# Attention with a one in the denominator, then a two-layer Mish block: how the first twelve head pairs and the first product are laid out

## The chip, the cores and the metric

The kernel runs on one core of one Trainium2 chip. The metric is the device time of one execution in microseconds; smaller is better. Three executions of the kernel before were timed. The profile is of one execution.

## The reference

`q`, `k` and `v` are 8 batches x 12 heads x 448 rows x 64, in float32; `w_in` is 768 x 2048 and `w_out` 2048 x 768.

```python
scores = scale * np.matmul(q, k.transpose(0, 1, 3, 2))
m = np.max(scores, axis=-1, keepdims=True)
e = np.exp(scores - m)
attn = e / (np.sum(e, axis=-1, keepdims=True) + np.exp(-m) + 1e-09)
attn_out = np.matmul(attn, v)
x = attn_out.transpose(0, 2, 1, 3).reshape(B * S, H * D)   # 3584 x 768
h = x @ w_in
sp = np.where(h > 20.0, h, np.log1p(np.exp(np.minimum(h, 20.0))))
out = (h * np.tanh(sp)) @ w_out                            # Mish, then the second product
```

## The kernel before

**Units of work.** Two heads make a pair: 6 pairs a batch, 48 pairs in all, numbered 0 to 47. Three pairs make a unit. The order of all instructions on each engine is written by hand: every engine takes its instructions in the order in which the Python code issues them, so a call made earlier stands earlier in that engine's queue.

**One pair.** `load_pair` issues three DMAs on SP's queue (L120). `cast_pair` makes bf16 copies on POOL (L161 to L163). `transpose_pair` turns q and k on PE (L178) into a PSUM tile, and `evac_qk` copies both out (L197 and L217 on ACT, or L199 and L215 on DVE; from pair 12 on, q goes out on DVE by L209 in a block-diagonal layout). Scores come in 4 steps a pair (`STEPS`), seven row tiles of 128 in all: two tiles in each of steps 0 to 2 and one in step 3. `scores` runs the matmuls (L254 to L265, later L248) into one of three score tiles in PSUM and then the negated row maximum on DVE (L269). `exps` runs the exponentials on ACT with their row sums (L282), and after a pair's last step a small exponential of the negated maxima (L289). `scores_ahead` keeps three steps in flight: the step that comes three later is issued after the exponentials of the present one have been issued, and uses the score tile that they free.

**Normalising and turning.** `denominators` (L295, L299, DVE) gives one over the sum; `normalise` multiplies the seven tiles in place, on DVE (L316), or on POOL (L314) after a copy of the factors (L307). The result must be turned before it is multiplied with v: by one DMA transpose on SP's queue (L320), or for the pairs in `BY_PE` by PE: `turn_on_pe(p, j)` does seven transposes (L331) into one of two PSUM tiles `mo`, and a DVE copy (L335) follows later. `av_pair` is the product with v (L357), its copy into `xT` (L366) again follows later. "Later" means a queue `late` in Python, emptied by `flush_late`, which issues the pending copies at that place. `mo_take` hands out the two `mo` tiles and empties `late` if none is free.

**The two products.** `mm1_mish` does six matmuls of `w_in` with `xT` (L381) for one of 16 blocks of 128 columns, then Mish on ACT (L387). The second product is dealt out in chunks of two matmuls (L436, `mm2_part`), which a unit's steps interleave with the scores; `plan` says which parts go into which unit. From unit 4 on (pair 12) each unit has such filler.

**Order before.** Pairs 0 to 5 run in a loop of their own, step by step, with no other PE work than attention. In it, at pair p: step 0 issues the loads of p+4, the casts of p+3, one piece of weights and the denominators of p-1; step 1 the copies of q and k of p+2 and the normalising of p-1 with its DMA transpose; step 3 the transposes of p+3 and the product with v of p-3. Then come units 2 and 3 (pairs 6 to 8 and 9 to 11), each followed by eight of batch 0's sixteen first-product blocks, with normalising, score steps and transposes of the next unit between them. Pairs 5, 6 and 7 are turned by PE, at most one turn a step. From unit 4 on the loop is the same to the end: twelve steps with filler of the second product, then eight blocks of a first product.

**Weights.** 20 pieces are loaded with a cast by DMAs that POOL issues (L147): 12 of `w_in` (256 rows x 512 columns each), 8 of `w_out`.

Of the kernel before, what the change touches and what calls it, by code (L numbers as in the profile page):

```python
# [19 lines left out]
def kernel(  # L20
# [15 lines left out]
    NT = 4  # L36
# [50 lines left out]
    for t_ in en_bufs:  # L87
# [140 lines left out]
    def scores(idx):  # L228

        p, s = divmod(idx, STEPS)  # L230
        if s == 0:
            if p < HP or p % UNIT_PAIRS == 0:
                for nm in ("negm", "sums", "expm", "den", "rden"):
                    stats[nm] = st_pool.tile([128, UNIT_PAIRS, NTILE], FP32, tag=nm, name=nm)
            at = 0 if p < HP else p % UNIT_PAIRS
            att[p] = {nm: t[:, at, :] for nm, t in stats.items()}
            att[p].update(en=en_bufs[p % N_EN], whole=dict(stats))
# [36 lines left out]
    def exps(idx):  # L274
# [6 lines left out]
        for bk, c in enumerate(cols):  # L281
# [5 lines left out]
            )  # L287
        if s == STEPS - 1 and p < HP:
# [12 lines left out]
    def normalise(p, dma=True, on_pool=False):  # L301
# [6 lines left out]
        for i in range(NTILE):  # L308
            args = dict(
                out=en[:, :, i, 0:SP_], in0=en[:, :, i, 0:SP_],  # L310
                scalar1=st["rden2" if on_pool else "rden"][:, i : i + 1],
            )
            if on_pool:
                nc.gpsimd.tensor_scalar(scalar2=1.0, op0=ALU.mult, op1=ALU.mult, **args)  # L314
            else:
                nc.vector.tensor_scalar(scalar2=None, op0=ALU.mult, **args)  # L316
        eT = eT_pool.tile([128, NT, 2 * S], BF16, tag="eT", name="eT")
        st["eT"] = eT
        if dma:
            nc.sync.dma_start_transpose(  # L320
                out=eT.rearrange("c j (i q) -> c (j i) q", q=128),
                in_=en.rearrange("q j i c -> q (j i c)"),
            )

    def turn_on_pe(p, j, act=False):
# [47 lines left out]

    def mm1_mish(b, ff):
        if ff == 0:
            gT[b] = gT_pool.tile([128, FF_T, S], BF16, tag="gT", name="gT")
        flush_late()
        spare = ff % FF_U == 2
        h_ps = sc_tiles[0][:, 0, :] if spare else mo_take()
# [97 lines left out]
    LOAD_AT = (0, 3, 6)  # L477
    HEAD = HP
# [13 lines left out]
    load_pair(3)  # L492
    cast_pair(2)


    for p in range(HEAD):
        for s in range(STEPS):
            if s == 1 and p == 0:
                transpose_pair(p + 2)
            exps(p * STEPS + s)  # L500
            if p == 0 and s == 0:
                evac_qk(1, act=True)
            if s == 1:
                evac_qk(p + 2, act=True)
            if s:
                flush_late()
            scores_ahead(HEAD * STEPS + 3)
            if s == (2 if p == HEAD - 1 else 0):
                load_pair(p + 4)
            if s == 0:  # L510
                cast_pair(p + 3)
                load_w(1)
                if p:
                    denominators(att[p - 1])
            if s == 1:
                if p:
                    normalise(p - 1)
            if s == 3 and p + 3 < HEAD + 2:
                transpose_pair(p + 3)
            if s == 3 and p >= 3:  # L520
                av_pair(p - 3, act=True)
    denominators(att[HEAD - 1])
    normalise(HEAD - 1, dma=HEAD - 1 not in BY_PE)

    for u in range(UNITS_PER_B, N_UNITS + 2 * UNITS_PER_B):
        attn = u < N_UNITS
# [9 lines left out]
        for n in range(steps):  # L536
            pi, s = divmod(n, STEPS)
            p, idx = p0 + pi, p0 * STEPS + n
            late_tp = u == UNITS_PER_B and n == STEPS
            if late_tp:  # L540
                transpose_pair(p0 + 2)
            exps(idx)
            if late_tp:
                evac_qk(p0 + 2)
            if u == UNITS_PER_B + 1 and n == 0:
                for j in range(2):
                    turn_on_pe(HEAD, j)
            flush_late()
# [10 lines left out]
            early = AV_AT.get(u - UNITS_PER_B)  # L559
            if early is not None:  # L560
                if n in early:
                    av_pair(early[n])
                for pe, n0 in BY_PE.items():
                    first = 2 if pe == HEAD else 0
                    if pe // UNIT_PAIRS == u - 1 and n0 + first <= n < n0 + NT:
                        turn_on_pe(pe, n - n0)
            elif s == (2 if pi else 0) and N_PAIRS <= p < N_PAIRS + UNIT_PAIRS:
                av_pair(p - UNIT_PAIRS)
            if u - UNITS_PER_B < len(W_AT):
                load_w(W_AT[u - UNITS_PER_B].get(n, 0))  # L570
        assert done == total
# [3 lines left out]
        nxt = p0 + UNIT_PAIRS  # L575
        todo = sorted(range(p0, nxt), key=lambda p: p in BY_PE)
        for f in range(FF_U):
            if moe:
                mm1_mish(b, w * FF_U + f)
            if u == UNITS_PER_B and f in (2, 6) or u == UNITS_PER_B + 1 and f == 1:  # L580
                load_w(1)
            if not attn:
                continue
            if f == 0:
                denominators(att[p0]["whole"])
                normalise(todo[0], dma=todo[0] not in BY_PE)
            if f == 3:
# [6 lines left out]
            if f == 3:  # L594
                normalise(todo[1], dma=todo[1] not in BY_PE)
            if f == (4 if u >= first_mm2 else FF_U - 1):
                normalise(todo[2], dma=todo[2] not in BY_PE, on_pool=u >= first_mm2)
    flush_late()
# [31 lines left out]
```

## Time and profile before

| | us |
|---|---|
| median of 3 runs (494.7 to 497.88) | 496.76 |
| profiled execution: its time and its span | 494.7 |
| PE busy (share of the span) | 453.2 (92%) |
| PE weight loads busy | 249.9 (51%) |
| DVE busy | 349.8 (71%) |
| ACT busy | 349.1 (71%) |
| POOL busy | 151.1 (31%) |
| share of the 16 DMA engines: SP's queue, POOL's queue | 80.7%, 8.8% |

The page's chain of what ended last goes through PE for 72% of the span, DVE for 12% and ACT for 10%. Busy times are shares of the whole span; what limits a stretch has to be read from that stretch. The first exponential starts at 7.9 us, that of pair 6 at 46.7, of pair 9 at 79.7 and of pair 12 at 111.6.

### The profile page before, as it was taken

The numbers are of one execution on the slowest core, as the hardware profiler recorded it, in microseconds if no ns is written. First come the engines' busy times: TensorE is split into PE (matmuls) and PEld (weight loads), VectorE is DVE, ScalarE is ACT, GpSimd is POOL, SyncE is SP. The second block draws the span as 40 slices with busy tenths as digits, with TensorE's granted clock in tenths as the row PEclk, the third lists the DMA queues.
The fourth block names the chain that finished last, engine by engine and source line by source line (L and its number), as shares of the span: only waits on it lengthen the run. The fifth ranks groups of instructions, "written<-read, shape, count | busy, mean of one in ns | idle before, by whom it ended". The sixth has DMA issues, their size and how long they took to land.

```text
span 494.7 us, 9027 instructions
## 1 busy us (share of the span) xinstructions
PE 453.2 (92%) x3120; PEld 249.9 (51%) x3120; DVE 349.8 (71%) x706; ACT 349.1 (71%) x906; POOL 151.1 (31%) x252
## 2 busy tenths in 40 slices
PE   4466877798999999999999999999999999999996
PEld 2122433454554556555655555555555565556573
DVE  4897988788868686968878786878796878420011
ACT  5888766668787787978797878888797879502300
POOL 4622271501432424242423324242424230300000
PEclk9999997799999999999999999999999999999999
DMA  8999999979999969989998999899989696670112
GB/s 209 194 213 228 243 222 226 193 135 217 192 218 286 184 201 189 264 163 233 195 242 188 191 193 218 221 179 245 194 243 181 187 146 144 128 159 18 47 50 79
DMA packets 209453, 92.20 MB, mean 186 GB/s; under 512 B 166272, under 2 KB 205952, under 8 KB 209408
## 3 DMA queue, kind: packets, MB, share of 16 engines
q1 hardware_dynamic: 201920, 85.35, 80.7%
q0 software_dynamic: 7488, 6.29, 8.8%
q8 instruction: 24, 0.39, 0.3%
q14 instruction: 21, 0.17, 0.1%
HBM read 45.61 MB, written 11.01 MB: 114 GB/s over the span
## 4 chain that ended last, share of the span: by engine, by line
PE 72%; DVE 12%; ACT 10%; issue 2%; DMA 1%; SPq 1%; POOL 0%; DVEq 0%; ACTq 0%; POOLq 0%
PE mo L436 24%; PE mo L381 24%; ACT en L282 9%; PE sc L248 8%; DVE negm L269 6%; PE sc L357 6%; DVE en L316 3%; PE sc L381 3%; PE sc L178 3%; PE mo L357 2%; DMA k_f<-in_k_dram 1%; PE sc L254 1%; DVE xT L366 1%; PE mo L331 1%; SPq L120 1%
## 5 line engine op out<-in xcount | busy, mean ns | idle before, releaser
L282 ACT ACTIVATE en<-sc,negm 128x448 bf16<-128x448 f32 x336 | 209.2, 636 | 33.6 <-DVE negm L269 15.3
L269 DVE TENSOR_REDUCE negm<-sc 128x2 f32<-128x896 f32 x192 | 182.9, 970 | 58.4 <-PE sc L248 44.4
L436 PE MATMUL mo<-w_out_sb,gT 128*128 128x384 bf16 (+2 forms) x1152 | 167.1, 309 | 0.0
L381 PE MATMUL mo<-xT,w_in_sb 128*128 128x448 bf16 x672 | 139.8, 352 | 1.3 <-DVE xT L366 1.0
L436 PEld LDWEIGHTS <-gT 128*128 128x128 bf16 (+1 forms) x1152 | 97.3, 100 | 56.5 <-issue 5.9
L387 ACT ACTIVATE gT<-mo 128x448 bf16<-128x448 f32 x112 | 59.3, 543 | 72.6 <-PE mo L381 72.4
L381 PEld LDWEIGHTS <-w_in_sb 128*128 128x128 bf16 x768 | 72.8, 98 | 64.6 <-issue 3.7
L314 POOL TENSOR_SCALAR en<-en,rden 128x448 bf16<-128x448 bf16 x84 | 51.8, 637 | 103.4 <-DVE rden L307 69.6
L161 POOL CAST q_bf<-q_f 112x512 bf16<-112x512 f32 x47 | 28.9, 614 | 155.2 <-DMA q_f<-in_q_dram 145.8
L422 DVE COPY o_sb<-mo 128x384 f32<-128x384 f32 (+1 forms) x64 | 32.1, 502 | 60.1 <-PE mo L436 60.0
L248 PE MATMUL sc<-kT,qd 128*128 128x448 bf16 x252 | 71.7, 354 | 1.5 <-DVE qd L209 0.7
L316 DVE TENSOR_SCALAR en<-en,rden 128x448 bf16<-128x448 bf16 x252 | 69.8, 348 | 0.9
L282 ACT ACTIVATION_READ_ACCUMULATOR en<-sc,negm 128x1 f32 x336 | 69.1, 206 | 0.0
L248 PEld LDWEIGHTS <-qd 128*128 128x128 bf16 x252 | 23.5, 97 | 33.3 <-issue 16.6
L254 PE MATMUL sc<-kT,qd 64*128 64x448 bf16 x36 | 17.5, 502 | 20.4 <-ACT en L282 17.4
L357 PE MATMUL sc<-eT,v_bf 112*64 112x448 bf16 x288 | 34.0, 356 | 2.3 <-ACT en L282 1.8
L163 POOL CAST v_bf<-v_f 112x512 bf16<-112x512 f32 x48 | 29.8, 621 | 14.3 <-DMA v_f<-in_v_dram 13.4
L357 PEld LDWEIGHTS <-v_bf 112*64 112x64 bf16 x384 | 21.3, 115 | 22.8 <-issue 16.8
L162 POOL CAST k_bf<-k_f 112x512 bf16<-112x512 f32 x47 | 29.0, 617 | 5.8 <-DMA k_f<-in_k_dram 5.1
L209 DVE TENSOR_SCALAR qd<-sc 64x448 bf16<-64x448 bf16 x72 | 27.8, 386 | 0.9
L217 ACT COPY kT<-sc 128x448 bf16<-128x448 bf16 x39 | 20.8, 535 | 8.2 <-PE sc L178 8.2
L178 PEld LDWEIGHTS <-q_bf 112*128 112x128 bf16 x192 | 14.4, 104 | 16.5 <-DVE q_bf L161 4.2
(47 smaller groups left out, 275.0 us busy)
## 6 DMA issues: line engine op xcount, KB each, us to landing
q_f<-in_q_dram SPq DMA_DIRECT2D x48, 224.0 KB, 5.1
k_f<-in_k_dram SPq DMA_DIRECT2D x48, 224.0 KB, 5.2
v_f<-in_v_dram SPq DMA_DIRECT2D x48, 224.0 KB, 5.4
w_in_sb<-in_moe_w_in_dram POOLq DMA_DIRECT2D x12, 256.0 KB, 5.6
w_out_sb<-in_moe_w_out_dram POOLq DMA_DIRECT2D x8, 384.0 KB, 7.4
out_dram<-o_sb SPq DMA_DIRECT2D x7, 336.0 KB, 3.6
out_dram<-o_sb SPq DMA_DIRECT2D x8, 288.0 KB, 4.6
out_dram<-o_sb SPq DMA_DIRECT2D x8, 240.0 KB, 3.2
```

Of the source, the lines that this page charges most:

```text
L163: nc.gpsimd.tensor_copy(out=v_bf, in_=v_f)
L178: nc.tensor.transpose(by_s[s][:, t * SP_ : (t + 1) * SP_], src[:, t].rearrange("p h d -> p (h d)"), ident[:SP_, :SP_],)
L248: nc.tensor.matmul(sc[:, bk, 0:S], lhsT=qT[:, i].rearrange("d h r -> d (h r)"), rhs=kT, start=True, stop=True,)
L269: nc.vector.tensor_reduce(out=negm, in_=sc[:, 0 : len(cols), 0:S], axis=AX.X, op=ALU.max, negate=True)
L282: nc.scalar.activation(out=st["en"][:, :, c, 0:SP_], in_=sc[:, bk, 0:S].rearrange("q (j c) -> q j c", j=NT), func=AF.Exp, bias=st["negm"][ ...
L314: nc.gpsimd.tensor_scalar(scalar2=1.0, op0=ALU.mult, op1=ALU.mult, **args)
L316: nc.vector.tensor_scalar(scalar2=None, op0=ALU.mult, **args)
L357: nc.tensor.matmul(av[h * 64 : (h + 1) * 64, 0:S], lhsT=v_bf[:, h, j * D : (j + 1) * D], rhs=e_h, start=(j == 0), stop=(j == NT - 1),)
L381: nc.tensor.matmul(h_ps[:, 0:S], lhsT=w_in_sb[:, dm, ff * 128 : (ff + 1) * 128], rhs=xT[b][:, dm, :], start=(dm == 0), stop=(dm == DM_T - 1),)
L387: nc.scalar.activation(out=gT[b][:, ff, :], in_=h_ps[:, 0:S], func=AF.Mish)
L422: nc.vector.tensor_copy(out=o_sb[:, cols], in_=st["o"][:, 0:n_cols])
L436: nc.tensor.matmul(st["o"][r : r + n, 0:n_cols], lhsT=gT[bb][:, ff, c0 : c0 + n], rhs=w_out_sb[:, ff, cols], start=(ff == 0), stop=(ff == ...
```

## The change

The loop of the first pairs now takes twelve pairs (`HEAD = 2 * HP`), and the general loop starts at unit 4. After pair 6 (`MOE_AFTER`) all sixteen blocks of batch 0's first product run in one stretch; the first two, which need all of `xT`, are begun with five of six matmuls each before pair 5's product with v (`mm1_first`). The pairs turned by PE are 3, 4, 5, 7 and 8, two turns in each of steps 2 and 3 of the next pair. Normalising of pair p-1 is dealt out: tiles 4 to 6 to POOL and tiles 0 and 1 to DVE in step 0, tiles 2 and 3 to DVE in step 1. The transposes of q and k of pair p+3 move from step 3 to step 1 of pair p, their copies by ACT to step 2 of pair p. One part of the second product (16 matmuls) is spread over the steps of pairs 10 and 11, and `plan` of units 4 and 5 is cut accordingly. `w_in` comes in pieces of 128 rows x 1024 columns; the places where pieces are issued are a table by pair and step.

```diff
+    HEAD = 2 * HP
...
     def w_pieces():
-        c_in, c_out = d_ff // 4, NH
-        for i in range(4):
-            for a in range(0, DM_T, 2):
+        c_in, c_out = d_ff // 2, NH
+        for i in range(2):
+            for a in range(DM_T):
                 yield (
-                    w_in_sb[:, a : a + 2, i * c_in : (i + 1) * c_in],
-                    moe_w_in[a * 128 : (a + 2) * 128, i * c_in : (i + 1) * c_in],
+                    w_in_sb[:, a : a + 1, i * c_in : (i + 1) * c_in],
+                    moe_w_in[a * 128 : (a + 1) * 128, i * c_in : (i + 1) * c_in],
                 )
...
+    def normalise_tiles(p, tiles, on_pool=False):
+        st = att[p]
+        en = st["en"]
+        if on_pool:
+            st["rden2"] = st_pool.tile([128, NTILE], FP32, tag="rden2", name="rden2")
+            nc.vector.tensor_copy(out=st["rden2"], in_=st["rden"])
+        for i in tiles:
+            ...
+            if on_pool:
+                nc.gpsimd.tensor_scalar(scalar2=1.0, op0=ALU.mult, op1=ALU.mult, **args)
+            else:
+                nc.vector.tensor_scalar(scalar2=None, op0=ALU.mult, **args)
...
+    def mm1_first(b, banks, last):
+        gT[b] = gT_pool.tile([128, FF_T, S], BF16, tag="gT", name="gT")
+        def part(ff, dms):
+            ...
+        for ff in range(len(banks)):
+            part(ff, range(DM_T - 1))
+        last()
+        flush_late()
+        for ff in range(len(banks)):
+            part(ff, (DM_T - 1,))
+            nc.scalar.activation(out=gT[b][:, ff, :], in_=banks[ff][:, 0:S], func=AF.Mish)
...
         if g == 0:
-            plan[u0] = [(0, i, 0, 2) for i in range(2)] + [(0, 2, 0, 1)]
-            plan[u0 + 1] = [(0, 2, 1, 1)] + [(0, i, 2, 2) for i in range(3)]
+            plan[u0] = [(0, i, 0, 2) for i in (1, 2)]
+            plan[u0 + 1] = [(0, i, 2, 2) for i in range(3)]
...
-    BY_PE = {HEAD - 1: 1, HEAD: 0, HEAD + 1: STEPS}
-    AV_AT = {0: {5: 3, 7: 4, 10: 5}, 1: {3: 8, 6: 6, 10: 7}}
-    W_AT = ({5: 1, 9: 1}, {1: 1, 5: 1, 7: 1, 9: 1, 11: 1}, {1: 1, 3: 1, 5: 1, 7: 1})
+    MOE_AFTER = HP
+    BY_PE = (3, 4, 5, 7, 8)
+    ON_POOL = 3
+    W_AT = {
+        (1, 2): 1, (2, 0): 1, (2, 2): 1, (3, 0): 1, (3, 2): 1, (4, 0): 1, (4, 2): 1,
+        (5, 0): 1, (5, 2): 1, (6, 0): 1, (6, 2): 2,
+        (7, 0): 1, (8, 0): 1, (8, 2): 1, (9, 0): 1, (9, 2): 1, (10, 0): 1, (10, 2): 1,
+        (11, 0): 1,
+    }
...
+    av_with.update({p: p - UNIT_PAIRS for p in range(MOE_AFTER + 3, HEAD)})
+    early = deque(fn for fn, _ in mm2_part(0, 0, 0, 2))
     for p in range(HEAD):
         for s in range(STEPS):
...
             exps(p * STEPS + s)
-            if p == 0 and s == 0:
-                evac_qk(1, act=True)
-            if s == 1:
-                evac_qk(p + 2, act=True)
-            if s:
-                flush_late()
-            scores_ahead(HEAD * STEPS + 3)
-            if s == (2 if p == HEAD - 1 else 0):
-                load_pair(p + 4)
-            if s == 0:
-                cast_pair(p + 3)
-                load_w(1)
-                if p:
-                    denominators(att[p - 1])
-            if s == 1:
-                if p:
-                    normalise(p - 1)
-            if s == 3 and p + 3 < HEAD + 2:
-                transpose_pair(p + 3)
-            if s == 3 and p >= 3:
-                av_pair(p - 3, act=True)
+            if p == 0 and s < 2:
+                evac_qk(1 + s, act=True)
+            if s == 2:
+                evac_qk(p + 3, act=True)
+            flush_late()
+            if p >= HEAD - 2:
+                early.popleft()()
+            limit = MOE_AFTER + 1 if p <= MOE_AFTER else HEAD + 1
+            scores_ahead(limit * STEPS)
+            load_w(W_AT.get((p, s), 0))
+            if s == 0:
+                load_pair(p + 4)
+                if p - 2 in BY_PE and p <= MOE_AFTER:
+                    av_pair(p - 2, act=True)
+                if p and p - 1 != MOE_AFTER:
+                    denominators(att[p - 1])
+                    normalise_tiles(p - 1, range(NTILE - ON_POOL, NTILE), on_pool=True)
+                    normalise_tiles(p - 1, range(0, 2))
+                cast_pair(p + 3)
+            if s == 1:
+                if p and p - 1 != MOE_AFTER:
+                    normalise_tiles(p - 1, range(2, NTILE - ON_POOL))
+                    turn(p - 1, dma=p - 1 not in BY_PE)
+                transpose_pair(p + 3)
+            if s >= 2 and p - 1 in BY_PE:
+                for j in (2 * s - 4, 2 * s - 3):
+                    turn_on_pe(p - 1, j)
+            if s == 3 and 3 <= p < MOE_AFTER and p - 3 not in BY_PE:
+                av_pair(p - 3, act=True)
+        if p == MOE_AFTER:
+            denominators(att[p])
+            mm1_first(
+                0, [sc_tiles[1][:, i, :] for i in range(2)],
+                lambda: (flush_late(), av_pair(p - 1, bank=sc_tiles[2][:, 0, :])),
+            )
+            normalise(p)
+            for ff in range(2, FF_T):
+                mm1_mish(0, ff, banks=False)
+                if ff >= FF_T - 6 and ff % 2 == 0:
+                    scores_ahead((p + 1) * STEPS + (ff - FF_T) // 2 + 4)
     denominators(att[HEAD - 1])
-    normalise(HEAD - 1, dma=HEAD - 1 not in BY_PE)
+    normalise(HEAD - 1)
...
-    for u in range(UNITS_PER_B, N_UNITS + 2 * UNITS_PER_B):
+    for u in range(first_mm2, N_UNITS + 2 * UNITS_PER_B):
```

`turn` is the part of `normalise` after the multiplications: it takes the tile `eT` and issues the DMA transpose if asked to.

More of the change, by code (lines that the diff above doesn't have):

```diff
@@ L287, in exps @@
             )
-        if s == STEPS - 1 and p < HP:
+        if s == STEPS - 1 and p < HEAD:
             nc.scalar.activation(out=st["expm"], in_=st["negm"], func=AF.Exp)
@@ L316, in normalise, with turn @@
                 nc.vector.tensor_scalar(scalar2=None, op0=ALU.mult, **args)
+        turn(p, dma)
+    def turn(p, dma):
+        st = att[p]
         eT = eT_pool.tile([128, NT, 2 * S], BF16, tag="eT", name="eT")
@@ L371, in av_pair, with mm1_mish @@
         del att[p], casted[p], qkT[p]
-    def mm1_mish(b, ff):
+    def mm1_first(b, banks, last):
+        gT[b] = gT_pool.tile([128, FF_T, S], BF16, tag="gT", name="gT")
+        def part(ff, dms):
+            for dm in dms:
+                nc.tensor.matmul(
+                    banks[ff][:, 0:S],
+                    lhsT=w_in_sb[:, dm, ff * 128 : (ff + 1) * 128],
+                    rhs=xT[b][:, dm, :],
+                    start=(dm == 0), stop=(dm == DM_T - 1),
+                )
+        for ff in range(len(banks)):
[5 more added lines that the diff above has]
+            nc.scalar.activation(out=gT[b][:, ff, :], in_=banks[ff][:, 0:S], func=AF.Mish)
+    def mm1_mish(b, ff, banks=True):
         if ff == 0:
@@ L377, in mm1_mish @@
         flush_late()
-        spare = ff % FF_U == 2
+        spare = banks and ff % FF_U == 2
         h_ps = sc_tiles[0][:, 0, :] if spare else mo_take()
@@ L558 @@
                 cast_pair(p0 + LOAD_AT.index(n) + LEAD - 1)
[L559 to L567, printed above, removed]
+            if s == (2 if pi else 0) and N_PAIRS <= p < N_PAIRS + UNIT_PAIRS:
                 av_pair(p - UNIT_PAIRS)
-            if u - UNITS_PER_B < len(W_AT):
-                load_w(W_AT[u - UNITS_PER_B].get(n, 0))
         assert done == total
@@ L585 @@
                 denominators(att[p0]["whole"])
-                normalise(todo[0], dma=todo[0] not in BY_PE)
+                normalise(p0)
             if f == 3:
@@ L594 @@
             if f == 3:
[L595 to L597 removed]
+                normalise(p0 + 1)
+            if f == 4:
+                normalise(p0 + 2, on_pool=True)
     flush_late()
```

26 lines of the change are left out of this document (10 added, 16 removed).

## The prediction

> **What bounds the kernel now.** The program runs on one core and its span of 494.7 us is the time of its profiled execution; the three runs lie at 494.7, 496.76 and 497.88 us, so the sum below is made against 494.7 and 2.1 us are added at the end for the median. First I read the stretches (columns: stretch, its length, busy time of PE, PE weight loads, DVE, ACT, POOL with counts, granted clock, DMA share, GB/s).
>
> ```profile
> 7.90:46.70 38.80, 22.24 (x119) 8.63 (x116) 32.05 (x63) 34.15 (x107) 15.79 (x25) 1.00 1.12 211
> 65.70:79.70 14.00, 11.13 (x86) 6.11 (x85) 11.54 (x25) 8.34 (x16) 6.69 (x11) 1.00 1.12 179
> 111.60:126.70 15.10, 13.04 (x88) 7.25 (x87) 12.60 (x23) 13.62 (x44) 4.29 (x7) 1.00 1.01 227
> 138.60:494.70 356.10, 350.32 (x2464) 197.57 (x2462) 236.09 (x473) 246.71 (x628) 101.21 (x168) 1.00 0.83 178
> ```
>
> From 138.6 us on PE is busy for 350.32 of 356.10 us: nothing lost earlier can be made up there. Before that PE is idle for much of the time, and every microsecond won or lost ahead of the first exponential of pair 12 (111.6 us) shows at the end. The change rewrites just this part. I call the time from the first exponential of pair p to that of pair p+1 "stage p". In the timeline stages 0 to 5 start at 7.9, 14.7, 20.0, 26.8, 32.7, 40.3 us, pairs 6 to 8 take 46.7 to 65.7, pairs 9 to 11 79.7 to 99.4, and the two halves of the first product 14.0 and 12.2 us. A stage thus costs 6.4 us on average.
>
> Second, the timeline of stage 3, for what hangs on what:
>
> ```profile
> 26.80 0.67 ACT L282 ACTIVATE en<-sc,negm 128x448 bf16<-128x448 f32 x1
> 28.25 0.58 PE L262 MATMUL sc<-kT,qd 64*64 64x448 bf16 x1
> 29.93 0.54 ACT L197 ACTIVATE qd<-mo 128x448 bf16<-128x448 bf16 x1
> 30.11 0.15 DVE L295 SCALAR_TENSOR_TENSOR den<-sums,expm 128x7 f32<-128x7 f32 x1
> 30.30 0.20 DVE L299 RECIPROCAL rden<-den 128x7 f32<-128x7 f32 x1
> 31.02 0.61 POOL L161 CAST q_bf<-q_f 112x512 bf16<-112x512 f32 x1 [9.33 <-DMA q_f<-in_q_dram]
> 33.29 0.56 PE L178 MATMUL mo<-ident,q_bf 112*128 112x112 bf16 x4
> ```
>
> The denominators of pair 2 are ready 3.7 us into stage 3 (2.7 us into stage 1, at 17.40, where no turn or normalising was pending), since on DVE they stand behind the maximum of the stage's last scores, and these wait for a score tile that the stage's first exponentials free. POOL's casts wait for the load alone, and the transposes made from them are copied out by ACT only in the next stage: there is a slack of half a stage. Stages 1 to 3 are DVE's (the chain from 20 to 48 us is 24.7% L269 and 23.3% L316).
>
> **What the change does to a plain stage.** Part one: normalising is dealt out, four tiles to DVE, three to POOL. On DVE that saves three tiles of 0.26 us and adds the 0.16 us copy (L307): DVE falls to 3.7 of maxima, 0.35 and 0.16 of denominators and 1.0 of tiles, 5.2 us. But POOL's three tiles are written ahead of the casts of pair p+3 in POOL's order, and the transposes of p+3 move from step 3 to step 1 and their copies by ACT from the next stage to step 2 of the same one. What was slack is now a chain inside each stage, and ACT, which takes its work in order, stands in it. Rows for the pieces:
>
> ```profile
> 16.17 0.58 PE L262 MATMUL sc<-kT,qd 64*64 64x448 bf16 x1
> 134.55 0.16 DVE L307 COPY rden<-rden 128x7 f32<-128x7 f32 x1
> 134.88 4.33 POOL L314 TENSOR_SCALAR en<-en,rden 128x448 bf16<-128x448 bf16 x7 [6.80 <-ACT kT L217]
> 16.55 0.62 POOL L162 CAST k_bf<-k_f 112x512 bf16<-112x512 f32 x1
> 15.65 0.58 PE L178 MATMUL mo<-ident,k_bf 112*128 112x112 bf16 x4
> 30.36 0.54 ACT L217 COPY kT<-mo 128x448 bf16<-128x448 bf16 x1
> ```
>
> Two exponentials release PE after 1.4 us (12.80 to 14.21); scores 0.55 and hand-over 0.15; maximum 0.6; denominators 0.3; copy and hand-over 0.3: 3.3 us. POOL: 3 x 0.62 = 1.85; casts of q and k 1.2: 6.35. PE turns k (0.55), ACT copies it (0.1 + 0.4): 7.4; last exponential and the small one 0.7: **8.2 us**, 1.8 more than a stage costs now. ACT would otherwise have come to the copies at 3.7 us; it stands idle for some 3 us. Nothing covers this: PE's next scores are queued behind the late transposes.
>
> **Turning by PE.** Pairs 3, 4, 5, 7 and 8 get 4 x 7 PE transposes and four DVE copies each in place of one DMA transpose (before: 5, 6, 7, spread one turn a step). Rows for a turn, a copy and one pair's product with v, at the slow and at the fast pace of PE:
>
> ```profile
> 53.46 0.99 PE L331 MATMUL mo<-ident,en 128*112 128x128 bf16 x7
> 54.08 0.61 DVE L335 COPY eT<-mo 112x896 bf16<-112x896 bf16 x1
> 59.28 1.68 PE L357 MATMUL mo<-eT,v_bf 112*64 112x448 bf16 x8
> 61.37 0.95 PE L357 MATMUL mo<-eT,v_bf 112*64 112x448 bf16 x8
> 89.18 0.60 PE L331 MATMUL mo<-ident,en 128*112 128x128 bf16 x7
> ```
>
> The turns stand in steps 2 and 3, behind the transposes of p+3; their copies stand on DVE ahead of two maxima, and a product with v stands on PE ahead of the next stage's last scores. So they lengthen the stage after, 5, 6, 9 and 10, from one stage's transposes to the next stage's: at the slow pace PE's scores, two turns, scores, two turns, product, scores (0.55 + 2.0 + 0.55 + 2.0 + 1.7 + 0.55 = 7.35), maximum 0.75, denominators, copy and hand-overs 0.65, POOL 1.85, casts 1.25, transposes 0.55: 12.4 us. At the fast pace DVE carries it (scores 0.45, maximum 1.05, copies 1.2, maximum 1.05, one copy 0.6, then product 0.95, scores and maximum 1.1, and from the denominators on the same with transposes of 0.36, 4.1): 10.5 us. Which pace PE has is not to be read from the granted clock, which is 1.00 in both 50 to 60 us and 60 to 70 us, but from the durations. In this part most are slow (L254 502 ns on average, 350 where fast). I take 11.6 us.
>
> The Trainium skill, "TensorE: Matmul & The Clock Gate" (Part 4: PE-mode transpose), says that transposes don't count as PE work in releasing the full clock; by it the five turns would stay at the slow pace and these stages at 12.4 us, 3.2 us more in all. The trace leaves it open: seven took 0.99 us at 53.46 and 0.60 at 89.18, among fast matmuls.
>
> The DMA side gains (six DMA transposes ahead of pair 12 in place of eight, loads no longer behind them on SP's queue), but in the longer stages each load has landed well before its cast: POOL's 35.2 us of waiting for q_f go into the new wait. I count nothing; if that cover went, it would cost as now, 1 to 2 us in a stage.
>
> **The first product in one stretch.** It needs 96 matmuls as before. From the end of pair 6's exponentials: remaining turns 1.2 to 2.8 us, ten matmuls 2 to 3, the product of pair 5 and its copy 1.7, two matmuls 0.4, fourteen groups of 1.14 (L381: six in 1.14 to 1.30) 16.0, three scores 1.1, last Mish and table load 1.9 (109.75 to 111.63 now): 24 to 27, taken 26, against 14.0 + 12.2 = 26.2. One pair of table loads goes, but ACT has room there. Normalising pair 6 (1.8 us of DVE) hides under it.
>
> **w_in in rows of 1024.** Still 12 pieces of 256 KB, 0.73 us each to issue on POOL, where POOL waits for the denominators anyway; w_out's eight follow, three of them earlier than now. Nothing; if POOL were full, 0.7 us a piece.
>
> **The sum.** Lead-in 7.9; stage 0 8.1 (6.8 and the copies of pair 3, which wait for its k cast at 14.2); stages 1 to 3 and 8 at 8.2: 32.8; stage 4 9.0 (ACT waits for pair 0's product with v); 5, 6, 9, 10: 46.4; stage 7 5.4 (no normalising in it); stage 11 9.6 (pair 8's product with v goes first, 0.95 to 1.7); stretch 26: 145.2 against 111.6, **+33.6**. Later, sixteen 384-column matmuls (2.6 us) move out of the PE-bound part and two narrow passes become one wider: 1.8 us less in each of two units, of which the first is ACT's (13.62 of 15.10 busy): -1.8 to -3.6, taken -2.4. Together +31.2: 525.9, with 2.1 **528 us**.
>
> **Rivals.** (1) PE stays fast throughout: 42 for the four long stages, plain ones 7.8, stretch 24.5, lower bounds elsewhere: +24.9 - 3.4, 518 us. For it: 89 to 91 us; against: fast spells last 2 to 4 us there. (2) PE slow throughout, and POOL and DVE hold each other up: +40 in all, 537 us. For it: seven DVE tiles took 1.80 us at 25.86 and 2.72 at 19.05, while POOL cast; that is 0.13 a tile, 0.5 a stage. The Trainium skill, "SBUF — State Buffer" (Who interferes with whom), has the two share a port pair that one holds for a whole instruction; by it POOL's three tiles could wait for two of DVE's, also 0.5 us a stage. (3) The other side: casts don't hold ACT up. It decides at 3.7 us into a stage: if k's copy can start by then, six plain stages run at ACT's 5.6 us, the five with a turn at 6.4 (19.0 / 3 now), stretch 24.5: 106.1, -5.5 - 2.4: 489 us. For it: DVE's load falls and it bounds stages 1 to 3; against: POOL's order, and 6.35 us of measured pieces ahead. (4) The loss vanishes in slack later: 497 us; against it the 350.32 of 356.10.
>
> **Numbers.** Chances: forecast 0.58, (1) 0.20, (2) 0.12, (3) 0.06, (4) 0.04. About 1% can be told from no change; the first three are slower by more, so slower 0.90, (4) same, (3) faster. The range runs from under rival 1, where two of its stages might go at less than DVE's sum, to rival 2: 512 to 538.
>
> **What would show it.** Pair 12's first exponential near 145 us; POOL casts right behind three L314-like tiles; ACT idle about 3 us a stage ahead of its copies, released by PE's transposes; long stages 5, 6, 9, 10; PE full after pair 15. Wrong if casts run ahead of denominators, if stages 1 to 3 stay under 7 us, or the stretch under 22.

## The result, and the profile after

Four runs of the changed kernel have a median of 537.17 us (535.98 to 538.17), four of the kernel before 496.19 us. The ratio is 1.0814, its 95% interval 1.0785 to 1.0843: **slower by 41 us**. The forecast was 528, its range 512 to 538. The profiled execution took 537.87 us with a span of 536.1; the sums below go by the spans, 536.1 against 494.7. (In every run that has both numbers the time is about 1.8 us above the span. The prediction took before's span for a time and added 2.1 us for the median, which comes to nearly the same.)

The stretches of the changed kernel, in the columns of the stretches shown of before: pairs 0 to 6, the stretch of the first product, pairs 7 to 11, unit 4, and the rest.

```profile
7.85:76.30 68.45, 34.91 (x228) 18.68 (x228) 41.31 (x78) 42.07 (x128) 34.24 (x57) 0.94 0.97 167
76.30:102.39 26.09, 22.81 (x128) 11.59 (x127) 7.88 (x16) 11.38 (x20) 2.68 (x5) 0.95 0.99 190
102.39:151.07 48.68, 29.14 (x174) 14.80 (x174) 34.51 (x70) 25.65 (x83) 20.76 (x33) 0.64 0.54 88
151.07:168.00 16.93, 14.86 (x81) 7.09 (x81) 14.52 (x26) 13.59 (x45) 3.61 (x6) 0.92 0.86 202
180.00:536.10 356.10, 349.26 (x2455) 196.87 (x2453) 236.36 (x472) 246.56 (x628) 101.46 (x168) 1.00 0.80 177
```

The last line says what the forecast needed: the PE-bound part is as full as before (349.26 of 356.10 us), so the early loss shows at the end. Pair 12's first exponential stands at 151.07 us; before it stood at 111.63. Of 41.4 us of span, 39.4 are lost ahead of it and 2.0 behind. In 7.85 to 76.30 no engine is full; ACT is busy for 61%. That is the picture of a chain. Its links, in the timeline of stage 2:

```profile
24.40 0.64 ACT L283 ACTIVATE en<-sc,negm 128x448 bf16<-128x448 f32 x1
25.80 0.53 PE L263 MATMUL sc<-kT,qd 64*64 64x448 bf16 x1 [0.77 <-ACT en L283]
26.48 0.62 DVE L270 TENSOR_REDUCE negm<-sc 128x1 f32<-128x448 f32 x1 [0.26 <-PE sc L266]
27.45 0.17 DVE L335 COPY rden<-rden 128x7 f32<-128x7 f32 x1
27.80 2.05 POOL L342 TENSOR_SCALAR en<-en,rden 128x448 bf16<-128x448 bf16 x3 [3.90 <-DVE rden L335]
29.80 0.64 POOL L162 CAST q_bf<-q_f 112x512 bf16<-112x512 f32 x1
30.40 0.60 POOL L163 CAST k_bf<-k_f 112x512 bf16<-112x512 f32 x1
31.06 0.55 PE L179 MATMUL mo<-ident,k_bf 112*128 112x112 bf16 x4
31.71 0.54 ACT L198 ACTIVATE qd<-mo 128x448 bf16<-128x448 bf16 x1 [3.50 <-PE mo L179]
32.15 0.53 ACT L218 COPY kT<-mo 128x448 bf16<-128x448 bf16 x1
33.28 0.64 ACT L283 ACTIVATE en<-sc,negm 128x448 bf16<-128x448 f32 x1
```

Each line starts within 0.2 us of the end of the one above, with three steps left out (the tile's second exponential, 25.00 to 25.65, the denominators from 27.02 on, and the pair's last exponential with the small one behind it, 32.56 to 33.28), and 8.9 us go by from one first exponential to the next. The bracket on L162 is missing: its load had long landed. The waits of 0 to 152 us (total, times, longest) show the same chain, and the one wait that the forecast lacked, the last. (POOL's longest, 32.6 us, is the stretch of the first product, where it has nothing to normalise.)

```profile
POOL en L342 <- DVE rden L335: 63.2, 7, 32.6
ACT qd L198 <- PE mo L179: 24.3, 9, 4.7
ACT kT L218 <- DVE qd L210: 19.1, 3, 6.8
```

| stage | forecast, us | measured, us |
|---|---|---|
| lead-in and 0 | 16.0 | 15.50 |
| 1, 2, 3, 8 | 8.2 each | 8.90, 8.88, 9.02, 8.97 |
| 4 | 9.0 | 9.64 |
| 5, 6, 9, 10 | 11.6 each | 13.50, 10.85, 11.27, 11.76 |
| stretch | 26 | 26.1 |
| 7 | 5.4 | 5.72 |
| 11 | 9.6 | 10.96 |
| sum to pair 12 | 145.2 | 151.07 |
| behind it, against before | -2.4 | +2.0 |

The lengths look right. Whether each has the cause that it was given is for the experiments. Where they give a stage's length, it runs from the small exponential that ends one pair (L290 in the changed kernel) to the next one.

### The profile page after: what moved, and what is told of

Read it like the earlier page. It is cut to its first block, busy times and chain, and to the rows that moved or that the text cites. A ratio compares the mean times of both kernels' runs of the same rounds, so it can differ in the third digit from the quotient of the medians.

```text
span 536.1 us, 9138 instructions
## 1 busy us (share of the span) xinstructions
PE 465.8 (87%) x3160; PEld 257.1 (48%) x3160; DVE 347.4 (65%) x694; ACT 350.1 (65%) x915; POOL 169.5 (32%) x282
## 4 chain that ended last, share of the span: by engine, by line
PE 67%; DVE 9%; ACT 9%; DMA 6%; POOL 4%; issue 3%; SPq 1%; DVEq 0%; POOLq 0%; ACTq 0%
PE mo L423 23%; PE mo L478 21%; PE sc L249 7%; ACT en L283 7%; PE sc L378 6%; DVE negm L270 5%; DMA k_f<-in_k_dram 4%; PE sc L423 3%; PE sc L179 2%; POOL en L342 2%; PE mo L179 1%; PE mo L352 1%; DVE xT L387 1%; DMA out_dram<-o_sb 1%; POOL q_bf L162 1%
## 5 line engine op out<-in xcount | busy, mean ns | idle before, releaser
L283 ACT ACTIVATE en<-sc,negm 128x448 bf16<-128x448 f32 x336 | 209.6, 640 | 21.1 <-DVE xT L387 10.8
L478 PE MATMUL mo<-w_out_sb,gT 128*128 128x384 bf16 (+2 forms) x1136 | 171.1, 314 | 0.5 <-DVE eT L356 0.5
L315 POOL TENSOR_SCALAR en<-en,rden 128x448 bf16<-128x448 bf16 x84 | 52.0, 641 | 102.8 <-DVE rden L308 69.2
L283 ACT ACTIVATION_READ_ACCUMULATOR en<-sc,negm 128x1 f32 x336 | 70.4, 210 | 0.0
L162 POOL CAST q_bf<-q_f 112x512 bf16<-112x512 f32 x47 | 29.1, 619 | 97.1 <-DMA q_f<-in_q_dram 71.1
L317 DVE TENSOR_SCALAR en<-en,rden 128x448 bf16<-128x448 bf16 x182 | 47.7, 334 | 0.8
L342 POOL TENSOR_SCALAR en<-en,rden 128x448 bf16<-128x448 bf16 x30 | 20.3, 687 | 80.4 <-DVE rden L335 63.2
L378 PE MATMUL sc<-eT,v_bf 112*64 112x448 bf16 x320 | 38.6, 362 | 3.0 <-ACT en L283 2.5
L179 PE MATMUL mo<-ident,q_bf 112*128 112x112 bf16 x60 | 8.1, 289 | 36.5 <-POOL q_bf L162 32.2
L179 PEld LDWEIGHTS <-q_bf 112*128 112x128 bf16 x192 | 14.4, 107 | 48.5 <-POOL q_bf L162 37.8
L164 POOL CAST v_bf<-v_f 112x512 bf16<-112x512 f32 x48 | 29.6, 618 | 16.0 <-DMA v_f<-in_v_dram 15.4
L163 POOL CAST k_bf<-k_f 112x512 bf16<-112x512 f32 x47 | 29.1, 619 | 5.3 <-DMA k_f<-in_k_dram 4.1
L255 PE MATMUL sc<-kT,qd 64*128 64x448 bf16 x36 | 18.0, 511 | 12.4 <-ACT en L283 11.8
```

Source lines behind the costliest of these rows:

```text
L162: cast_q(out=q_bf, in_=q_f.rearrange(by_t, t=NT))
L179: nc.tensor.transpose(by_s[s][:, t * SP_ : (t + 1) * SP_], src[:, t].rearrange("p h d -> p (h d)"), ident[:SP_, :SP_],)
L283: nc.scalar.activation(out=st["en"][:, :, c, 0:SP_], in_=sc[:, bk, 0:S].rearrange("q (j c) -> q j c", j=NT), func=AF.Exp, bias=st["negm"][ ...
L378: nc.tensor.matmul(av[h * 64 : (h + 1) * 64, 0:S], lhsT=v_bf[:, h, j * D : (j + 1) * D], rhs=e_h, start=(j == 0), stop=(j == NT - 1),)
L478: nc.tensor.matmul(st["o"][r : r + n, 0:n_cols], lhsT=gT[bb][:, ff, c0 : c0 + n], rhs=w_out_sb[:, ff, cols], start=(ff == 0), stop=(ff == ...
```

## The experiments

All edits are to the changed kernel but one. A run without an interval is a single execution, so 2 us between two of them tell nothing (before ran between 494.1 and 498.2); the stages, which start and end inside one execution, are compared instead.

**Casts ahead of POOL's tiles.** Theory: the chain within a stage is the loss. Rival: moving the turns and the products is.

```diff
                 load_pair(p + 4)
+                cast_pair(p + 3)
...
                     normalise_tiles(p - 1, range(0, 2))
-                cast_pair(p + 3)
```

> The changed kernel with one call moved: the casts of pair p+3 stand ahead of POOL's three normalising tiles in POOL's order; nothing else differs. Theory (the chain inside a stage: denominators, POOL's tiles, casts, transposes, ACT's copies): ACT no longer idles 3.5 us ahead of its copies in plain stages; stages 1, 2 and 8 fall from 8.9 us to about 6, stages 3 and 4, where the loads of pairs 6 and 7 come into play, to 7 or 8, the four long stages (13.5, 10.9, 11.3, 11.8) to 8 to 10, stage 11 from 11.0 to 8; pair 12's first exponential moves from 151 to about 126 and the time from 537 to about 512 us. Rival (the turning by PE carries the loss): stages 1, 2, 3 and 8 may shorten, but the long ones stay at 10 to 13 and the time stays over 525. Rival (the slow pace of PE alone): every stage stays within 1 us, over 530.

530.21 us. Stages 1, 2 and 8 fall to 5.72 us each: the chain was what set them. But stage 3 takes 14.1 us, and only 7 us of the whole are won. In the timeline of this kernel's SP and POOL:

```profile
21.67 7.53 SPq L325 DMA_TRANSPOSE eT<-en  x1
29.26 0.56 SPq L121 DMA_DIRECT2D q_f<-in_q_dram  x1
37.86 0.61 POOL L162 CAST q_bf<-q_f 112x512 bf16<-112x512 f32 x1 [9.58 <-DMA q_f<-in_q_dram]
```

The same DMA transpose in the changed kernel:

```profile
21.16 4.37 SPq L325 DMA_TRANSPOSE eT<-en  x1
```

The cast waits 9.58 us for a load of q. SP could issue that load only at 29.26 us, behind a DMA transpose that held the queue for 7.53 us in place of 4.37, and the cast could start only 8.6 us after that. A second limit stands behind the first.

**All seven tiles on DVE**, dealt out as in the change, so that nothing of POOL's stands ahead of the casts:

```diff
-                    normalise_tiles(p - 1, range(NTILE - ON_POOL, NTILE), on_pool=True)
...
-                    normalise_tiles(p - 1, range(2, NTILE - ON_POOL))
+                    normalise_tiles(p - 1, range(2, NTILE))
```

> The changed kernel with all seven normalising tiles on DVE (two in step 0, five in step 1): POOL has only casts and DMA issues in the first twelve pairs. Theory (the chain): the casts run as soon as their loads have landed, as when they are moved ahead; DVE takes 0.8 to 1.2 us more a stage, so plain stages come to 6 to 6.5 us and the long ones to 9 to 11; about 515. Rival (DVE's relief by POOL is worth more than POOL's order costs): slower than 537, DVE full. Rival (turning carries it): over 525.

528.1 us, 13 above the expectation. Stages 1 to 3 take 5.71, 6.71 and 7.05 us; stages 4 and 6 go up to 11.7 and 11.8, and POOL now waits for q_f. The same turn of events by another edit.

**Transposes late.** The transposes of p + 3 go back to step 3 and their copies to the next stage; POOL's order stays.

```diff
-            if s == 2:
-                evac_qk(p + 3, act=True)
+            if s == 1:
+                evac_qk(p + 2, act=True)
...
-                transpose_pair(p + 3)
...
+            if s == 3:
+                transpose_pair(p + 3)
```

> The changed kernel with the transposes of pair p+3 back in step 3 and their copies by ACT back in step 1 of the next pair; POOL's tiles still stand ahead of the casts. Theory (the chain needs both, POOL's order and the early copies): with the slack of half a stage back, ACT doesn't wait: stages 1 and 2 fall from 8.9 to 6 or 6.3 us although the casts are as late as in the changed kernel; from stage 3 on the loads decide (they waited behind 7.5 to 9.5 us of DMA transposes when the casts were put first), 7 to 9 us; pair 12 starts at 120 to 135 instead of 151, the time is 508 to 523 us. Rival (POOL's order alone costs, wherever the transposes stand): stages 1 and 2 stay over 8 us, over 530 in all.

543.3 us, outside the expectation, and still it answers the question: stages 1 to 3 take 5.27, 5.39 and 5.75 us. So the chain needs both halves, POOL's order and the early copies; undoing either breaks it. The time is lost elsewhere. Pair 9's transposes now hold one of the two `mo` tiles through the stretch, which takes some 36 us, a side effect of this edit. And stage 5 takes 21.4 us, from the waits of 40 to 70 us:

```profile
ACT en L283 <- DMA eT<-en: 12.0, 1, 12.0
```

Pair 5's exponentials wait for pair 1's DMA transpose to leave their buffer; SP's row for it is 17.41 us long.

**w_in in rows of 512**, as before:

```diff
-        c_in, c_out = d_ff // 2, NH
+        c_in, c_out = d_ff // 4, NH
...
-                    w_in_sb[:, a : a + 1, i * c_in : (i + 1) * c_in],
+                    w_in_sb[:, a : a + 2, i * c_in : (i + 1) * c_in],
```

> The changed kernel with w_in in pieces of 256 rows x 512 columns again, issued at the same places. In the changed kernel the loads of pair 8 reached POOL late in stage 5 (2.5 us of waiting), while the DMA engines were busy at only 65 to 105 GB/s. Theory (the chain): the pieces cost nothing in plain stages; the time stays within 2 us of 537. Rival (the long rows crowd the loads): stage 5 falls from 13.5 to about 11 and the time to 534 or 535; if the rows carried the loss, below 525.

535.58 us: the rows cost nothing that shows. Stage 5 takes 10.8 us in it, but also 11.1 and 11.2 in two later runs that keep the long rows; the 13.50 of the profiled execution was that execution's.

**w_in not loaded.** If the crowded transfers are the second limit, taking w_in's twelve away must free stage 3 once the casts go first, and change nothing while the chain stands. Two kernels, both with

```diff
+    nc.vector.memset(w_in_sb[:, 0:4], 0.02)
+    nc.gpsimd.memset(w_in_sb[:, 4:DM_T], 0.02)
...
-                yield (
-                    w_in_sb[:, a : a + 1, i * c_in : (i + 1) * c_in],
...
+                yield None
```

the first with the casts moved as above, the second without:

> The casts stand ahead of POOL's three tiles, and w_in is not loaded: DVE and POOL set it to a constant at the start, so the values are others, and twelve transfers of 256 KB are gone. Theory: with the chain in a stage undone, the loads are the next limit, and w_in is what crowds them. Then stage 3 (14.1 us with the casts first and w_in loaded) falls under 8, stage 5 (12.8) under 10.5, POOL's wait for q_f from 29.1 us under 10, SP's DMA transposes go back from 7.5-9.5 to under 6 us each, and the time from 530.2 to 517-523 us. Rival: what is left is the order of work on DVE and PE: stages 3 and 5 stay above 12 and the time within 3 us of 530.

> The changed kernel with its order kept, and w_in not loaded (set to a constant, as in the run beside it). Theory: in the changed kernel the chain inside a stage ends last and the loads have slack behind it, so the plain stages stay at 8.8-9.0 us; only stage 5 may lose 2 us, and the time is 533-537 us. Rival: crowded transfers also lengthen the plain stages: they fall under 8 us and the time under 528.

By the end of stage 0 the memsets have put the whole back by 4.9 us in the first, beside the run with the casts moved, and by 5.3 us in the second, beside the changed kernel; that is taken off here. Since stage 0 ends between 15.4 and 16.8 us in the runs of this order that load w_in, the corrected times are good to about 1 us. The first: 524.8 - 4.9 = **519.9 us**. Stage 3 falls from 14.1 to 5.97 us, stage 5 from 12.8 to 10.8; POOL's wait for q_f falls only from 29.1 to 22.5 us (13.7 of it in one), where under 10 was expected. SP's DMA transposes of pairs 0 to 2 take 4.3 to 5.9 us, where they took 7.5 to 9.5 with w_in.

The second: 541.18 - 5.3 = 535.9 us, beside 537.2 with w_in. Stages 1 to 3 take 8.98, 9.02 and 9.02 us, and ACT waits 3.5 to 3.6 us in each, as with the loads; in stage 1:

```profile
28.18 0.55 ACT L200 ACTIVATE qd<-mo 128x448 bf16<-128x448 bf16 x1 [3.50 <-PE mo L181]
```

In the times both are as the theory has it: w_in is worth about 1 us in the changed kernel and 10.3 us as soon as the chain is gone. Each limit hides the other, and undoing one gives back only what the other leaves.

**No turns on PE.** `BY_PE` empty, five more DMA transposes; the products of pairs 3 and 4 move into pair 6.

```diff
-    BY_PE = (3, 4, 5, 7, 8)
+    BY_PE = ()
...
+            if p == MOE_AFTER and s in (0, 2):
+                av_pair(3 + s // 2, act=True)
```

> The changed kernel with no pair turned by PE: pairs 3, 4, 5, 7 and 8 go by DMA transpose, and the products with v of pairs 3 and 4 stand in steps 0 and 2 of pair 6. Theory (the chain is there in every stage, and the turns lengthen it in four): stages 5, 6, 9 and 10 fall from 13.5, 10.9, 11.3, 11.8 to about 9 to 10, plain stages stay at 8.9, the product of pair 5 may hold up the stretch by some us because its DMA transpose lands late: about 530. Rival (the turning carries the loss): pair 12 starts below 125 us, the time is under 512. Rival (the turning saves DMA time that the loads need): slower than 537, with POOL waiting for loads.

548.31 us. Stages 5 and 6 take 13.4 and 10.3 us, stages 9 to 11 take 10.96, 10.96 and 10.9: hardly shorter than with the turns. That doesn't clear the turns, since other work takes their place. A stage's denominators stand on DVE behind the maximum of its last scores (the single tile, L263), which PE reaches 1.4 us into a plain stage. In stage 9 of the changed kernel, from 117.08 us on, turns and a product with v stand ahead of them, and it is 3.5 us:

```profile
117.98 1.74 PE L352 MATMUL mo<-ident,en 128*112 128x128 bf16 x14
119.66 0.95 PE L378 MATMUL sc<-eT,v_bf 112*64 112x448 bf16 x8
120.53 0.37 PE L263 MATMUL sc<-kT,qd 64*64 64x448 bf16 x1
```

Without the turns stage 9 starts at 129.15 us, and the last scores still come at 3.0 us, because the same product now runs at the slow pace:

```profile
130.55 1.70 PE L378 MATMUL sc<-eT,v_bf 112*64 112x448 bf16 x8 [0.77 <-ACT en L283]
132.18 0.58 PE L263 MATMUL sc<-kT,qd 64*64 64x448 bf16 x1
```

In stage 5 the last scores come 2.2 us into the stage in place of 3.7, but POOL then waits 3.75 us for a load, which SP issued behind a DMA transpose of 7.32 us:

```profile
62.39 0.61 POOL L162 CAST q_bf<-q_f 112x512 bf16<-112x512 f32 x1 [3.75 <-DMA q_f<-in_q_dram]
```

So this run doesn't settle what the turns cost. The stretch takes 38 us, as its waits from 60 us on show: pair 5's DMA transpose comes late, its product with v later, and ACT's first Mish last, after a wait of 12.7 us.

```profile
DVE xT L387 <- PE sc L378: 15.4, 1, 15.4
```

Of the three views on record the last, that the turns save DMA time which the loads need, is the one that came out.

**The same with the chain and w_in gone** tells whether the turns were merely hidden (the diffs of the casts, of w_in and of the turns together):

> The casts ahead of POOL's tiles, w_in not loaded (a constant in its place, so the values are others), and no pair turned by PE: five more DMA transposes, with the products with v of pairs 3 and 4 moved into pair 6. The same kernel with the turns has 10.8 and 9.3 us in stages 5 and 6 and 11.75, 12.5 and 10.1 us in stages 9 to 11. Theory: under the chain inside a stage, which is gone here, the turns and their copies are the next thing that ends last: stage 5 falls to 7-8.5 us, stages 9 to 11 to 8.5-9.5 us, since DVE's copies of q still stand behind its tiles there. Rival: as with the chain in place, the turns cost under 0.8 us a stage: stage 5 stays over 10 and stages 9 to 11 over 10 on average. The stretch of the first product waits for the DMA transpose of pair 5 again: 27-38 us where the turns give 26.7.

531.4 us. Half of each view: stages 5 and 6 fall from 10.8 and 9.3 to 7.3 and 7.4 us, so there the turns cost 5.4 us together. Stage 9 falls from 11.75 to 10.1; stage 10 stays at 12.6, now with a wait of POOL for q_f of 7.59 us in it, and stage 11 goes from 10.1 to 11.1. The stretch goes from 26.7 to 36.8 us, since SP needs

```profile
61.31 18.96 SPq L327 DMA_TRANSPOSE eT<-en  x2
```

for pairs 5 and 6, and the first product needs pair 5. The turns thus save 10 us at the stretch, with no w_in to load, and cost 5.4 in stages 5 and 6 and 0.6 in stages 9 to 11 taken together.

**ACT's copy of k ahead of DVE's copies of q.** In stages 9 to 11 of the changed kernel ACT's copy of k waits for DVE's two copies of q, which read the same PSUM tile and stand behind four tiles of normalising:

```profile
124.16 1.01 DVE L344 TENSOR_SCALAR en<-en,rden 128x448 bf16<-128x448 bf16 x2
126.30 0.79 DVE L210 TENSOR_SCALAR qd<-mo 64x448 bf16<-64x448 bf16 x2 [0.56 <-PE mo L179]
127.20 0.53 ACT L218 COPY kT<-mo 128x448 bf16<-128x448 bf16 x1 [6.31 <-DVE qd L210]
```

k's transposes had ended before 126.30, so ACT lost 0.9 us by the order in which the two were issued.

```diff
+        if p >= DIAG_FROM and act:
+            nc.scalar.copy(kT, k_ps[:, 0:S])
         if p < DIAG_FROM:
```

> The changed kernel with one order changed for pairs 12, 13 and 14, copied out in stages 9, 10 and 11: ACT's copy of k is issued ahead of DVE's copies of q from the same PSUM tile. In the changed kernel ACT's copy starts only when DVE's have ended (127.09 to 127.20, 138.85 to 138.97, 149.81 to 149.92). Theory (two engines that read one PSUM tile go in the order of issue): stages 9, 10 and 11 shorten by 0.8 us each, pair 12 starts 2 to 2.5 us earlier. Rival (the copy waits for something else that DVE does): no change in the three stages.

535.77 us. Stages 9 and 11 fall to 10.41 and 10.14 us, by 0.86 and 0.82 as expected; stage 10 rises to 13.06. Right in two stages, given back in the third.

**A light start of unit 4**, which took 17.0 us and was forecast to get shorter:

```diff
-            acc += weight[n]
-            want = int(total * acc / sum(weight) + 1e-6)
+            share = [1.0] * steps if u == first_mm2 else weight
+            acc += share[n]
+            want = int(total * acc / sum(share) + 1e-6)
```

> The changed kernel with the filler of unit 4 spread evenly over its twelve steps, not 36% of it in the first. In the changed kernel unit 4 takes 17.0 us, from 151.1 to the small exponential at 168.0, against 15.1 before, and starts with twelve matmuls at the slow pace (3.1 us) ahead of the product and scores that ACT waits 2.6 us for. Theory (the heavy first step, which used to run while ACT loaded its table behind Mish, now stands in ACT's way): unit 4 falls to about 15 us, the time to 535. Rival (unit 4 is longer because PE is slow, wherever the filler stands): unchanged within 0.5 us. Stages 0 to 11 are as in the changed kernel either way.

536.7 us, unit 4 16.5 us, among 16.2 to 18.0 in the runs that leave unit 4 alone and keep the turns: the heavy first step is not the cause.

**Three parts undone at once** (casts first, transposes late, rows of 512):

> The changed kernel with three things undone at once: casts ahead of POOL's tiles, transposes in step 3 with copies in the next pair's step 1, and w_in in pieces of 256 rows x 512 columns. What stays is the order of pairs, the first product in one stretch, the five turns by PE and POOL's three tiles. Theory (chain plus loads): pair 12 starts at 115 to 125 us, the time is 500 to 512. If it stays above 520, the order of pairs with the single stretch or the turns cost by themselves, and the chain is not the main loss; if it falls below 496, they are worth having.

540.52 us. Stages 1 to 3 take 5.27, 5.39 and 5.55 us, stages 4 to 6 take 14.0, 14.4 and 12.0, with POOL waiting 25.6 us for q_f; stretch and unit 4 have the same side effect of late transposes as above. It expects under 512 if the parts add up. They don't. By its own words a time over 520 says that the order of the pairs or the turns cost by themselves and that the chain is not the main loss; this run can't carry that alone, since the waits for loads and a stretch of some 35 us are in the same time.

**The kernel before with one part of the change**, three tiles on POOL, behind the casts:

```diff
-                    normalise(p - 1)
+                    normalise(p - 1, on_pool=True, pool_from=4)
```

(`pool_from` leaves the tiles below it to DVE.)

> The kernel before with one thing of the change: in the first pairs three of the seven normalising tiles go to POOL, behind the casts, with the transposes and their copies where they were. Theory: stages 1 to 4 there are DVE's, each loses 0.62 us of DVE's work, and nothing waits for POOL's tiles but the DMA transpose; the time falls by 1 to 3 us, to 493-495. Rival: POOL waits up to 9 us for loads there, so its tiles and the DMA transpose behind them start late, hold up the loads queued behind it on SP, and it costs 2 to 8 us: 498-504.

Ten runs, median 497.02 us; ratio to before 1.0014, interval 0.9993 to 1.0035: no change. Pair 5's exponentials end 0.9 us earlier (45.52 against 46.41), pair 8's 0.4 us later (66.11 against 65.72). Neither view holds; a DVE with less to do gains nothing that lasts. No kernel tried beats before.

## Why the prediction came out as it did

**The sign, the PE-bound end and the chain of the plain stages: right.** The chain from denominators over POOL's tiles, casts and transposes to ACT's copies was forecast link by link. Two runs that break it at different links bring the plain stages from 8.9 to between 5.3 and 5.8 us. Rival 3, by which casts don't hold ACT up, fails at its own point of decision: ACT's copies start 7.3 us into stage 2, not 3.7. But of the 33.6 us that were forecast ahead of pair 12, 20.8 stood in the four long stages (11.6 in place of 6.4 us each), and there the sum was right in part by luck.

**A plain stage: mis-sized, 8.9 for 8.2.** Two terms. The sum let ACT copy q while PE turned k; ACT started only when both had been turned (31.71, behind 31.06 + 0.55), 0.45 us. And POOL's three tiles took 2.05 us, not 1.85. (The forecast's own pieces add up to 8.1.) The page's groups have both kinds of POOL tile, most with a tile of DVE's beside them (L342) and none with one (L315):

```profile
L315 POOL TENSOR_SCALAR en<-en,rden 128x448 bf16<-128x448 bf16 x84 | 52.0, 641 | 102.8 <-DVE rden L308 69.2
L342 POOL TENSOR_SCALAR en<-en,rden 128x448 bf16<-128x448 bf16 x30 | 20.3, 687 | 80.4 <-DVE rden L335 63.2
```

That is 46 ns a tile, 0.14 us a stage. Rival 2 had 0.5. The Trainium skill, "SBUF — State Buffer" (Who interferes with whom), with a port pair held for a whole DVE instruction, came to the same 0.5; this trace shows no wait of that size on POOL. It does show one on DVE, off the chain: two of its tiles took 0.96 us at 29.02, beside POOL's tiles and casts, and two took 0.57 us at 27.53.

**The long stages: 47.4 us for 46.4, by errors that cancel.** The forecast put turns and a product with v ahead of the last scores, at 3.4 us over a plain stage. They do stand there, but the last scores came only 2.1 to 2.6 us later than in a plain stage (3.5 to 4.0 us into the stage, not 1.4). What filled the gap was not in the sum: the 0.7 us by which a plain stage was mis-sized; in stages 9 and 10 the wait for DVE's copies of q, named above; and in stage 5 of the profiled execution 2.5 us in which POOL waits for loads (1.63 for q, 0.90 for k). The same wait for the copies of q is 0.8 of the 1.4 us by which stage 11 was over, for so much goes with the copy of k put first. It stands in every variant of the changed kernel but that one, and with the casts first it grows: in stage 9 of the run without turns and w_in, k has been turned 5.0 us into the stage, and DVE comes to its copies of q at 8.0, behind its maxima and tiles. What stages 9 to 11 would cost without it stays open, since no run brought their average under 10.4 us and none takes these copies off DVE.

**PE's pace.** The choice between 12.4 and 10.5 us hung on it, and both paces came up in one stage: the turns slow, the product behind them fast (0.95 us at 119.66). The granted clock, 1.00 in the windows of before that the prediction read, does show it here: 0.50 from 64.70 to 68.25, where PE does 23 transposes of turns and one pair of scores, and 0.91 from 68.25 to 69.50, the product behind them. The Trainium skill, "TensorE: Matmul & The Clock Gate" (Part 4: PE-mode transpose), has transposes not count; here the clock rose directly behind 3.5 us of little else. In the run with the casts first and w_in not loaded it stayed at 0.50 from 115.06 to 120.60, 2.4 us of that ordinary matmuls, and then rose. The first speaks against the rule and the second fits it, but doesn't need it: PE had no pause over 0.2 us for the last 5.3 us before the rise in the one and 5.9 in the other. Not settled.

**DMA "I count nothing": nearly right for this kernel, and the cover was named.** Only in stage 5 does the chain wait for loads, the 2.5 us above, and in three other runs with w_in and the same turns it takes 10.8 to 11.2 us in place of 13.5. The prediction priced the loss of that cover at 1 to 2 us a stage; with the casts first it was 8 us in one stage and 10.3 in all. Its reason, fewer DMA transposes, missed that a single stretch wants all of w_in within the first seven pairs, where before half of it could follow later.

**The stretch: right**, 26.1 for 26. What guards it is the turning of pairs 3 to 5 on PE, which the prediction counted only as a cost: without it the stretch is 10 to 12 us longer.

**Behind pair 12: wrong sign, +2.0 for -2.4.** The 1.8 us saved in each of two units came to 17.0 us in unit 4 in place of 15.1, and to 0.3 and 0.6 us won in units 5 and 6 and lost again at the end. The first filler ran fast in the kernel before, under the table load of the first product; now PE comes to it slow (0.85 granted from 151.07 to 160.00, 1.00 before from 111.6). The run with a light start doesn't bear out the rest of that reading, so it is argued, not shown.

**Rival 2's 537** is the number that came out, by other means: its PE was slow in much of this part (0.64 granted in pairs 7 to 11), but the four long stages took 47.4 us together and not four times 12.4, and POOL lost 0.14 us a stage, not 0.5. The 528 fell short by 5.9 us ahead of pair 12 (3.0 in the four plain stages, 1.4 in stage 11, 1.0 in the long ones) and 4.4 behind.

What the 41 us were, by the runs in a row: 7 go with the order of POOL's casts, 10 more with w_in, both by single executions. Of the 24 left in that kernel 14.7 lie in stages 9 to 11 (34.4 us, before 19.7; the late last scores and DVE's copies of q are what its rows show there, and no run takes both away), 6.5 in pairs 0 to 8 (5.4 of them the turns), the rest behind pair 12 and in the stretch.

## What to carry to other kernels

Before moving work earlier, ask in which engine's order it then stands and what it waits for there: an early transpose behind a late normalising tile turned half a stage of slack into a chain. When one fault is mended and little comes back, look at what waits next in the same stages; limits that lie on top of each other show singly only when the others are gone. A part that looks like a cost in its own stage can be what another stage lives on, so remove it alone and read both. When a stage stays as long without a part, look whether something else has moved into its place before calling the part harmless: compare the links, not the length alone.

## What the hardware showed that was not expected

- A DMA transpose of one pair holds SP's queue for 4.2 to 4.4 us when little else moves, and among loads of q, k, v and w_in for up to 17.4 us (7.53, 9.23 and 9.47 with the casts first, 17.41 with the transposes late); everything behind it on SP waits as long.
- ACT's and DVE's copies out of one PSUM tile ran one after the other in the order of issue, though they read different halves: 0.1 us from the end of the one to the start of the other, in stages 9 to 11. Whether the chip orders them so or the program's own waits do, no run here tells.
- Neither copy started before both q's and k's transposes into that tile had ended.
